# Two loads of v issued behind two transposes instead of ahead of them, on the queue of SyncE, in a fused attention and gated feed-forward kernel

## The chip, the core and the metric

The kernel runs on one core of a Trainium2 chip. The core has five engines that run their own instruction streams: TensorE (PE in the profile, its weight loads PEld), VectorE (DVE), ScalarE (ACT), GpSimd (POOL) and SyncE (SP), which here only issues transfers. Transfers run on 16 DMA engines. The metric is the device time of one execution in microseconds (us), lower is better.

## What is computed

Eight batches of eight heads, 576 tokens, head size 64: attention that is causal by blocks of 64 tokens, then a feed-forward layer with a ReLU gate over all 4608 tokens.

```python
scores = scale * np.matmul(q, k.transpose(0, 1, 3, 2))      # (8, 8, 576, 576)
mask = block_i >= block_j                                    # blocks of 64
scores = np.where(mask, scores, -1000000000.0)
attn = exp(scores - max) / sum
attn_out = np.matmul(attn, v)
x = attn_out.transpose(0, 2, 1, 3).reshape(4608, 512)
gate = np.maximum(x @ w_gate, 0.0)                           # 512 -> 1536
val = x @ w_val
out = gate * val @ w_out                                     # 1536 -> 512
```

## The kernel before

**Tiling.** A batch has 512 "main" tokens, four chunks of 128, and 64 "tail" tokens that are kept apart. Attention runs in rounds: round r is batch r // 4, head pair r % 4. A round computes the scores transposed (keys on the partitions, queries along the row), takes the exponential on ACT into `attnT`, and in the next round multiplies by v (`head_av`, L648). A column of ones beside v gives the sum for the normalisation. The rows are then turned for the feed-forward layer.

**Rounds and the feed-forward layer.** PE alternates between a round's attention and units of the feed-forward layer of an earlier batch. The generator `ffn_gen` yields after every few matmuls; `parts(n)` (L860) takes n such steps and `ffn(n)` (L847) whole units. So a `parts` or `ffn` call in the program is a stretch of PE work, and also ACT and DVE work that belongs to it.

**Order.** The whole body stands under a manual schedule for PE, DVE, ACT, POOL and SP: each engine runs its instructions in the order in which the program issues them. Where the program puts a call, it puts its instructions at that place of every engine that the call uses. An engine waits in order: an instruction that waits holds up all behind it on its engine.

**How batch 2 gets its data.** An object `Early(2)`, `e2`, loads through SP into float32 `stage` tiles (ten of them, handed out in turn, L186), POOL casts them to bf16, and transposes by DMA bring q and k into the form that the scores need:

- `e2.load_qk`, `e2.cast_qk`, `e2.transpose(0)` and `(1)` (L397): the main tokens of q and k, into `perm`, sorted by `unpermute` (L408) into `qTm` and `kTm`.
- `e2.load_tails((0, 1))`, `e2.cast_tails` (L334 and L336) and `e2.transpose_tails` (L439 and L440): the tail tokens of q and k, into `qTt[0]` and `kTt[0]`. Two transposes by DMA, issued by SP.
- `e2.load_tails((2,))` (L309): the tail tokens of v, two loads.
- `e2.load_v_chunks(0)` and `(1)` (L290): v of the main tokens, two loads of 256 KB each, in rows of 256 bytes. `e2.cast_v_chunks` (L349) on POOL puts them into `v_bf[0]` in round 8.

The first round of batch 2 is r = 8. Its `scores_all` reads `qTt[0]` in the last of its three pieces; `scores_last(2)` reads `kTt[0]` some steps later; `head_av(8, 0)`, in round 9, is the first to read the chunks of v. The same steps for batch 3 (`e3`) are issued in round 8, straight behind these on SP: loads of q and k, tails, chunks of v, transposes. Its tails go to `qTt[1]` and `kTt[1]`, first read in round 12. From batch 4 on POOL issues the loads (`load_qkv`, L460), which cast on the way.

PSUM has eight banks: three pairs are handed out in turn by `take`, two banks hold the products with v.

Of the kernel before, what the change touches and what calls it, by code (L numbers as in the profile page):

```python
# [17 lines left out]
def kernel(  # L18
# [581 lines left out]
    def tails_av(b, hh):  # L600

        av = banks[:, AV + hh, 0:260].rearrange("p (n d) -> p n d", d=65)
        for hp in range(4):
            for c in range(NCH):
                col = 1024 * hh + 256 * hp + 64 * c
                w = (
                    attnE[:, col : min(col + 128, 2048)]
                    if c < 4
                    else attnD[b % 2][:, 64 * hp : 64 * hp + 128]
                )  # L610
                nc.tensor.matmul(
                    av[0 : w.shape[1], hp, :],
                    w,
                    v_bf[b % 2][:, c, 2 * hp + hh, :],
                    start=(hp == 0 and c == 0),
                    stop=(c == 4),
                    skip_group_check=True,
                )
# [241 lines left out]
    def parts(n):  # L860

        for _ in range(n):
            next(gen)
            part[0] += 4
            done[0] += 4
# [14 lines left out]
    with tc.manual_schedule(engines={E.PE, E.DVE, E.Activation, E.Pool, E.SP}):  # L880
# [76 lines left out]
        e1, e2, tails = Early(1), Early(2), Tails()  # L957
# [75 lines left out]
        to_xT_pe(7, (dve,), banks[:, AV])  # L1033
        parts(1)
        e2.load_tails((2,))
        parts(2)
        e2.load_v_chunks(0)
        e2.load_v_chunks(1)
        parts(1)
        tails_av(0, 0)  # L1040
        tails_av(0, 1)
        tails_of(0, xt)
# [5 lines left out]
        e2.cast_tails((pool, pool))  # L1048
        parts(2)
        e2.transpose_tails()  # L1050
        parts(1)
        e2.unpermute(1, (dve, pool))
        for r in range(8, 4 * B):
# [79 lines left out]
```

## Time and profile before

| | |
|---|---|
| median of 3 runs | 368.88 us (367.63 to 368.9) |
| the profiled execution | 368.08 us, of which the span is 366.3 us |
| granted TensorE clock, mean | 0.998 |
| busy share of the span | PE 97%, DVE 45%, ACT 46%, POOL 31% |
| transfers | 51.02 MB in 136579 packets, 139 GB/s over the span |

The profile shows one execution. Times are us from the start of the span. A line of a time view gives start, length, engine, the line in the kernel, operation, tile written <- tile read, and the count of instructions; in brackets stands how long the engine was idle before it and what ended that. SPq, POOLq and ACTq are the queues of the engines that issue transfers; the length there is that of the issue, not of the transfer. Windows list, for each stretch, the busy time of PE, PEld, DVE, ACT and POOL, then the granted clock, the busy share of the DMA engines and GB/s; that share can go over 1, since several packets overlap on an engine. The share of the DMA engines by slice (40 slices of 9.2 us, in tenths) shows where transfers are dense:

```profile
PE   7899999989999999999999999999999999999995
POOL 5777854535888306800590032000000000000000
DMA  8999997799999999986899939173200130020013
GB/s 251 308 374 380 365 238 242 142 234 245 194 185 137 142 169 94 188 85 119 102 172 86 149 79 128 28 136 78 75 16 18 47 102 1 3 86 29 2 39 104
```

The place of the change is in slices 7 and 8 (64 to 82 us).

### The profile page before, as it was taken

Reading aid. Unit: us, or ns where it says so; the run is one execution under the profiler, and the core shown is the slowest. Engines: PE = TensorE matmul, PEld = TensorE weight load, DVE = VectorE, ACT = ScalarE, POOL = GpSimd, SP = SyncE. Lnnn points to the kernel's source line nnn. Section 1 sums busy time; section 2 is a strip of 40 time slices with the busy share of each in tenths; the row PEclk is TensorE's granted clock in tenths of the full one; section 3 lists DMA queues with packets and bytes.
Section 4 is the critical chain, followed back from the end, with each engine's and each line's share of the span. In section 5 each row is a group of like instructions: output and inputs, shape, how many; then the busy total and the mean of one; then the engine's idle time right before and its main releaser. Section 6 shows DMA issues by size and latency. Waiting matters only on the chain.

```text
span 366.3 us, 7450 instructions
## 1 busy us (share of the span) xinstructions
PE 354.4 (97%) x2944; PEld 187.6 (51%) x2983; DVE 165.7 (45%) x327; ACT 167.6 (46%) x266; POOL 112.9 (31%) x161
## 2 busy tenths in 40 slices
PE   7899999989999999999999999999999999999995
PEld 3544456545555455555555555555555544444443
DVE  4834446556465543444344443544344424333432
ACT  5924528456756653565346543654264303302310
POOL 5777854535888306800590032000000000000000
PEclk9999999999999999999999999999999999999999
DMA  8999997799999999986899939173200130020013
GB/s 251 308 374 380 365 238 242 142 234 245 194 185 137 142 169 94 188 85 119 102 172 86 149 79 128 28 136 78 75 16 18 47 102 1 3 86 29 2 39 104
DMA packets 136579, 51.02 MB, mean 139 GB/s; under 512 B 117472, under 2 KB 127456, under 8 KB 136544
## 3 DMA queue, kind: packets, MB, share of 16 engines
q1 hardware_dynamic: 74880, 34.29, 40.9%
q0 software_dynamic: 56384, 7.08, 37.0%
q10 hardware_dynamic: 5280, 9.18, 7.2%
q8 instruction: 23, 0.38, 0.5%
q14 instruction: 12, 0.10, 0.1%
HBM read 37.75 MB, written 9.44 MB: 129 GB/s over the span
## 4 chain that ended last, share of the span: by engine, by line
PE 85%; DMA 3%; issue 3%; POOL 2%; ACT 2%; SPq 2%; DVE 1%; POOLq 0%; DVEq 0%; ACTq 0%
PE banks L790 42%; PE banks L820 23%; PE banks L648 7%; PE banks L749 6%; PE banks L514 5%; DMA stage<-in_v_dram 2%; ACT attnT L520 2%; PE banks L869 1%; SPq L290 1%; DMA qTt<-q_bt 1%; POOL q_bf L316 1%; DVE xnat L593 1%; POOL k_bf L316 1%; PE banks L424 1%; PE banks L693 0%
## 5 line engine op out<-in xcount | busy, mean ns | idle before, releaser
L520 ACT ACTIVATE attnT<-banks 128x1024 bf16<-128x1024 f32 (+1 forms) x118 | 85.0, 805 | 56.2 <-PE banks L514 44.7
L799 ACT ACTIVATE gate_sb<-banks 128x512 bf16<-128x512 f32 x96 | 57.8, 603 | 93.0 <-PE banks L790 92.8
L820 PE MATMUL banks<-wo,hT 128*128 128x512 bf16 (+1 forms) x432 | 96.4, 373 | 1.0 <-ACT attnT L520 0.4
L804 DVE TENSOR_TENSOR hT<-gate_sb,banks 128x512 bf16<-128x512 bf16 x96 | 65.8, 687 | 69.8 <-PE banks L790 67.0
L790 PE MATMUL banks<-xT,wv 128*128 128x512 bf16 x331 | 86.6, 379 | 0.3
L790 PE MATMUL banks<-xT,wg 128*128 128x512 bf16 x319 | 85.9, 379 | 0.9
L820 PEld LDWEIGHTS <-hT 128*128 128x128 bf16 x444 | 42.4, 98 | 46.3 <-issue 0.5
L790 PEld LDWEIGHTS <-wv 128*128 128x128 bf16 x384 | 37.6, 98 | 45.2
L790 PEld LDWEIGHTS <-wg 128*128 128x128 bf16 x384 | 36.2, 98 | 40.2 <-issue 0.2
L832 DVE COPY ob<-banks 128x512 f32<-128x512 f32 (+1 forms) x37 | 25.0, 676 | 53.1 <-PE banks L820 53.0
L460 POOL DMA_DIRECT2D v_bf<-in_v_dram x16 | 14.5, 919 | 67.2 <-PE banks L648 66.6
L648 PE MATMUL banks<-v_bf,attnT 128*128 128x65 bf16 x792 | 33.2, 194 | 0.0
L648 PEld LDWEIGHTS <-attnT 128*128 128x128 bf16 x792 | 29.0, 98 | 7.3 <-issue 0.6
L514 PE MATMUL banks<-qTm,kTm 64*128 64x512 bf16 (+3 forms) x256 | 24.8, 299 | 1.7 <-ACT attnT L520 1.1
L593 DVE TENSOR_TENSOR xnat<-banks,recip 128x640 bf16<-128x640 f32 (+2 forms) x35 | 25.8, 737 | 1.4 <-DVE recip L592 0.2
L514 PEld LDWEIGHTS <-kTm 64*128 64x128 bf16 x512 | 17.1, 94 | 12.8 <-issue 4.7
L592 DVE RECIPROCAL recip<-banks 128x10 f32<-128x10 f32 (+3 forms) x37 | 7.8, 211 | 32.8 <-PE banks L648 29.7
L460 POOL DMA_DIRECT2D k_bf<-in_k_dram x16 | 14.3, 911 | 1.6 <-DMA v_bf<-in_v_dram 1.6
L460 POOL DMA_DIRECT2D q_bf<-in_q_dram x16 | 14.4, 934 | 0.0
L579 DVE MEMSET attnT<- 64x192 uint32 x25 | 5.5, 218 | 19.4 <-ACT attnT L520 16.4
L763 DVE TENSOR_TENSOR hT<-gate_sb,banks 128x512 bf16<-128x512 bf16 x12 | 7.7, 683 | 13.6 <-PE banks L749 13.6
L790 PE MATMUL banks<-xTt,wg 128*128 128x512 bf16 x48 | 12.3, 379 | 0.1
(104 smaller groups left out, 250.1 us busy)
## 6 DMA issues: line engine op xcount, KB each, us to landing
out_dram<-ob ACTq DMA_DIRECT2D x32, 256.0 KB, 2.3
stage<-in_moe_w_gate_dram SPq DMA_DIRECT2D x6, 512.0 KB, 9.0
stage<-in_moe_w_val_dram SPq DMA_DIRECT2D x6, 512.0 KB, 9.8
stage<-in_q_dram SPq DMA_DIRECT2D x6, 512.0 KB, 6.8
stage<-in_k_dram SPq DMA_DIRECT2D x6, 512.0 KB, 8.1
stage<-in_moe_w_out_dram SPq DMA_DIRECT2D x6, 512.0 KB, 10.5
stage<-in_v_dram SPq DMA_DIRECT2D x8, 256.0 KB, 4.8
q_bf<-in_q_dram POOLq DMA_DIRECT2D x16, 128.0 KB, 6.3
```

The lines of the kernel that those rows point to most:

```text
L460: nc.gpsimd.dma_start(dst, src[b, :, 128 * c : 128 * c + n, :].rearrange("h p d -> p h d"),)
L514: nc.tensor.matmul(o, kTm[b % 2][ps, c, hp, :], x, start=True, stop=True)
L520: nc.scalar.activation(out, sc, AF.Exp, scale=scale)
L592: nc.vector.reciprocal(recip, av[:, :, :, 64])
L593: nc.vector.tensor_tensor(out=out, in0=av[:, :, :, 0:64], in1=recip.to_broadcast([rows, heads, n, 64]), op=AX.mult,)
L648: nc.tensor.matmul(av[:, 0, p, :], w, vb[:, c, h, :], start=(p == 0), stop=(c == p), skip_group_check=True,)
L749: nc.tensor.matmul(out[key][:, f % 2, :], (wg, wv)[t][i][:, c, fo : fo + 128], x[:, c, :], start=(c == 0), stop=(c == 3),)
L790: nc.tensor.matmul(out[f][:, t, :], (wg, wv)[t][i][:, c, fo : fo + 128], x[:, c, :], start=(c == 0), stop=(c == 3),)
L799: nc.scalar.activation(gate[f], out[f][:, 0, :], AF.Relu)
L804: nc.vector.tensor_tensor(out=h, in0=gate[f], in1=out[f][:, 1, :], op=AX.mult)
L820: nc.tensor.matmul(ops[:, g, 0 : n1 - n0], hT[f][:, 128 * s : 128 * (s + 1)], wo[i][:, f % 4, n0:n1], start=(f == 0), stop=(f == 11),)
L832: nc.vector.tensor_copy(ob, ops[:, g, 0 : n1 - n0])
```

## The change

Batch 2's two calls that load v in chunks move behind the call that transposes its tails. The stretches of PE work around them are the same: `parts(2)` and `parts(1)` become `parts(3)`.

```diff
         e2.load_tails((2,))
-        parts(2)
-        e2.load_v_chunks(0)
-        e2.load_v_chunks(1)
-        parts(1)
+        parts(3)
         tails_av(0, 0)
...
         e2.cast_tails((pool, pool))
         parts(2)
         e2.transpose_tails()
+        e2.load_v_chunks(0)
+        e2.load_v_chunks(1)
         parts(1)
         e2.unpermute(1, (dve, pool))
         for r in range(8, 4 * B):
```

The functions that these calls reach:

```python
def load_v_chunks(self, g):
    st = self.st["c", g] = new_stage(1024)
    for i in range(2):
        s0 = 256 * g + 128 * i
        nc.sync.dma_start(
            st[:, 512 * i : 512 * i + 512].rearrange("p (h d) -> p h d", h=8),
            v[self.b, :, s0 : s0 + 128, :].rearrange("h p d -> p h d"),
        )
...
def transpose_tails(b, q_t):
    nc.sync.dma_start_transpose(qTt[b % 2], q_t)
    nc.sync.dma_start_transpose(
        kTt[b % 2], k_bt[b % 2].rearrange("p h n -> p (h n)")
    )
```

All six transfers are issued by SP. No other engine's stream changes.

## The prediction

> **What bounds the kernel now.** I read the page first, then the waits of the matmul engine, then the chain of waits around the place of the change, and last the transfers.
>
> ```profile
> span 366.3 us, 7450 instructions
> PE 354.4 (97%) x2944; PEld 187.6 (51%) x2983; DVE 165.7 (45%) x327; ACT 167.6 (46%) x266; POOL 112.9 (31%) x161
> PE 85%; DMA 3%; issue 3%; POOL 2%; ACT 2%; SPq 2%; DVE 1%; POOLq 0%; DVEq 0%; ACTq 0%
> ```
>
> ```profile
> PE banks L514 <- DMA qTt<-q_bt: 1.6, 1, 1.6
> ```
>
> PE is busy for 354.4 of 366.3 us. The line by itself is the whole answer to "what did PE wait for from 76 us to the end": one wait, for batch 2's qTt. After it the chain of work runs through PE alone. So time can be won behind 76 us only at that one wait, and an end of the kernel can move later only if something new stops PE.
>
> ```profile
> 61.08 0.90 PE L514 MATMUL banks<-qTt,kTm 64*128 64x64 bf16 x32
> ...
> 76.30 0.72 PE L514 MATMUL banks<-qTm,kTm 64*128 64x512 bf16 x8
> 78.59 0.29 PE L514 MATMUL banks<-qTt,kTm 64*128 64x64 bf16 x8 [1.57 <-DMA qTt<-q_bt]
> ...
> 85.18 0.59 PE L648 MATMUL banks<-v_bf,attnT 128*128 128x65 bf16 x14
> ...
> 105.64 0.28 PE L514 MATMUL banks<-qTt,kTm 64*128 64x64 bf16 x8
> ```
>
> This is PE in order of time (start, length, line, operation). The scores of round 8 begin at 76.30 and run out of work at 77.02; the eight matmuls on batch 2's tail queries start at 78.59, after 1.57 us idle. 85.18 is the first product with batch 2's v. 105.64 is the same eight matmuls of batch 3.
>
> ```profile
> 67.14 0.41 POOL k_bt L336
> ...
> 70.11 1.73 SPq L290
> ...
> 73.13 1.28 SPq L290
> ...
> 74.58 3.96 DMA qTt<-q_bt
> ```
>
> The chain of waits says why. The cast that the transposes need ends on POOL at 67.55, but SP comes to them only at 74.58, because the v chunks (L290) stand ahead from 70.11.
>
> ```profile
> 68.76 1.31 SPq L309 DMA_DIRECT2D stage<-in_v_dram  x2
> 70.11 4.30 SPq L290 DMA_DIRECT2D stage<-in_v_dram  x4
> 74.58 1.69 SPq L439 DMA_TRANSPOSE qTt<-q_bt  x1
> 76.38 1.20 SPq L440 DMA_TRANSPOSE kTt<-k_bt  x1
> 77.62 0.58 SPq L257 DMA_DIRECT2D stage<-in_q_dram  x1
> ...
> 97.95 1.43 SPq L439 DMA_TRANSPOSE qTt<-q_bt  x1
> 99.48 2.22 SPq L440 DMA_TRANSPOSE kTt<-k_bt  x1
> ```
>
> SP's queue: two tail loads of v, four chunk loads, the two transposes of batch 2, then the loads of batch 3; its two tail transposes come at 97.95 and 99.48. Time from issue to landing, in this order: the last chunk load, the two transposes of batch 2, batch 3's first load of q, the two transposes of batch 3.
>
> ```profile
> stage<-in_v_dram SPq DMA_DIRECT2D x1, 256.0 KB, 5.0
> qTt<-q_bt SPq DMA_TRANSPOSE x1, 4.0
> kTt<-k_bt SPq DMA_TRANSPOSE x1, 2.6
> stage<-in_q_dram SPq DMA_DIRECT2D x1, 512.0 KB, 4.1
> qTt<-q_bt SPq DMA_TRANSPOSE x1, 6.3
> kTt<-k_bt SPq DMA_TRANSPOSE x1, 8.1
> ```
>
> **The change, part by part.** No instruction is added or removed. On SP four loads and two transposes trade places; the order of every other engine stays, and so does the order in which stage buffers are handed out, so no load gets another buffer to wait for.
>
> *The transposes, moved up.* They need the casts (over at 67.55) and the old qTt read out (the row at 61.08, over by 62). Neither is late at 70.11, so SP issues them there, right behind the v tails. From 74.58 to 77.62 the pair took 3.04 us with its gaps. Landing is 2.6 to 6.3 us behind the issue by the nearest rows; I take 4.0, which had the chunk loads ahead, so 74.1, and 76.4 at the worst. Both lie ahead of 77.02, so this wait goes whole: **1.57 us**. Matmuls behind it need nothing else that is late: ACT's exponentials are further down.
>
> The Trainium skill, DMA: Bandwidth & Descriptors, section Queues, rings and completion order, says that a DMA's semaphore increment is a strongly ordered write that lands only after every earlier write of that engine. By that rule qTt's landing carried the chunk loads ahead of it, and the trace agrees as far as kTt's 2.6 is shorter than qTt's 4.0; with 2.6 the landing would be at 72.7, and the sum the same.
>
> *The chunk loads, moved down.* First issue 70.11 + 3.04 = 73.15. From the first issue to the last landing they took 73.13 + 5.0 - 70.11 = 8.0 us, so the last lands at 81.2. Below that: the first issue took 1.73 us of SP where an even share of the four is 1.08; without that excess 80.5. Above: with batch 3's transposes as the measure (97.95 to 101.70, 3.75 us), 81.9. Then POOL casts:
>
> ```profile
> 78.22 1.04 POOL L349 CAST v_bf<-stage 128x1024 bf16<-128x1024 f32 x1 [1.13 <-DMA stage<-in_v_dram]
> 81.82 1.04 POOL L316 CAST q_bf<-stage 128x1024 bf16<-128x1024 f32 x1 [2.56 <-DMA stage<-in_q_dram]
> ```
>
> 81.2 + 0.1 + 1.04 = 82.3 (81.6 to 83.0). The first v product, moved up by the gain, stands at 85.18 - 1.57 = 83.6. The cover is 1.3 us (0.6 to 2.0): no cost. Without cover each microsecond would cost one. POOL's next cast, 81.82 before, starts some 0.5 later, and catches up in POOL's gaps.
>
> *ACT.* Its last exponential of round 8 cannot move up by the whole 1.57:
>
> ```profile
> 78.92 1.02 ACT L520 ACTIVATE attnT<-banks 128x1024 bf16<-128x1024 f32 x1 [0.19 <-PE banks L514]
> ```
>
> It waited 0.19 only, since ACT had the earlier ones to do until 78.73, and so ends at 79.75 instead of 79.94. ACT can then be 1.57 - 0.19 = 1.38 us behind PE's new pace at most. PE feels a late gate only when it wants that unit's pair of banks again, and there are three pairs: no cost.
>
> *What is late next: batch 3.* Its loads start behind the same six transfers, and SP reaches them at the same 77.62 (77.62 is 70.11 + 4.30 + 3.04 with gaps, in either order). What changes is what the DMA engines still have to do then.
>
> ```profile
> 78.00:79.00 1.00, 0.41 (x14) 0.36 (x14) 0.00 (x0) 0.81 (x2) 0.78 (x1) 1.00 0.47 73
> 79.00:80.00 1.00, 1.00 (x21) 0.77 (x19) 0.14 (x1) 0.94 (x1) 0.26 (x1) 1.00 0.23 62
> 80.00:81.00 1.00, 0.95 (x6) 0.43 (x5) 0.93 (x3) 0.21 (x1) 0.00 (x0) 1.00 1.08 383
> ```
>
> The last three columns are PE's granted clock, the DMA engines' share and GB/s. The engines had room at 78 to 80 (0.47, 0.23), and ran full from 80 with batch 3's loads. In the changed kernel the chunks, landing by 81.2, fill that room, and batch 3's first load comes behind them: 512 KB at 383 GB/s is 1.4 us, so it lands at about 82.1 if its data follow at 80.7, against 77.62 + 4.1 = 81.7 before. Call this shift s: 0.4. With chunks at 80.5 it is zero; if nothing of the room were used, it would be the whole 3.04.
>
> It matters because PE now comes earlier to batch 3's tails. qTt landed at 97.95 + 6.3 = 104.25 and was read at 105.64: 1.39 spare. kTt landed at 99.48 + 8.1 = 107.6 and its weights were loaded at 108.7:
>
> ```profile
> L551 PEld LDWEIGHTS <-kTt x4: 97/98/98, 108.7 to 109.0; 128*128 128x128 bf16 x4
> ```
>
> That is 1.10 spare. A PE that is 1.57 ahead uses both up. With s = 0.4: qTt at 104.65 against 104.07, PE waits 0.58; kTt at 108.0 against 107.71, it waits 0.29. Kept: 1.57 - 0.58 - 0.29 = **0.70**; in general 1.10 - s, and never over 1.57. Later rounds gave no wait before, and I see none that 0.7 us would make.
>
> **Sum.** The profiled execution took 368.08 (366.3 its span); minus 0.7 is 367.4. The shown median, 368.88, lies 0.8 above it (runs from 367.63 to 368.9). I take the middle of the two, 368.4, as the time before: **367.7**.
>
> **Rivals.** (1) *The whole 1.57 is kept*: batch 3's tails land earlier than worked out, since chunks need less than 8.0 us behind the shorter transposes, or since the loads that POOL issues for batch 4 come at another moment. For it: those transposes took 6.3 and 8.1 with POOL's transfers beside them, 4.0 and 2.6 without. Against: both queues start later by the same late landings. Time 366.8.
>
> (2) *Slower*: the late chunks push all of batch 3, and its tail transposes become the new, longer wait of PE at 105.64 and 108.7. For it: the engines run full from 80 us, and 8.1 against 2.6 shows what neighbours cost a small transpose there. Against: the room at 78 to 80 is 0.53 + 0.77 = 1.3 us of the engines, to set against the 3.04. It decides from s = 1.1; with the whole 3.04 the kernel loses 3.04 - 1.10 = 1.9, time 370.3.
>
> The skill's same page, Rules for kernel authors, advises to issue a DMA early and to wait on it late; for the chunks and all behind them the change does the reverse. With 3.04 us given up to 1.3 of cover at the v products, the trace does not bear that out here as a loss; by the rule the time would be that of (2) or (3).
>
> (3) *PE waits for the v chunks* instead, at the product of 85.18. With the cast over at 84.1 it would wait 0.5, and batch 3 takes no more than before, since PE has then 1.07 of lead, within the spare of 1.10: 367.3. For a loss the last chunk must land at 84.1, 6 us later than before, and no row gives that.
>
> That the change does not do what it says I exclude: the cast is over 2.6 us before SP is free.
>
> **Numbers.** Forecast 0.50; whole gain 0.20; batch 3 late 0.24; chunks late 0.06. The forecast's own range, for s from 0 to 0.8, is 367.3 to 368.1, and with the spread of the runs 367.0 to 368.6. The 8-in-10 range goes to both neighbours: 366.4 (whole gain with a fast base) to 369.7 (s of some 2.4). A half per cent, 1.8 us, is about what a measurement of this kernel can tell from no change. Faster by over that: most of the whole gain when the time before is at 368.9 (0.14), the forecast's edge (0.07), some of (3): 0.22. Slower by over that: the far part of (2), 0.20. Within: 0.58.
>
> **What would show it.** In the changed profile: SP issues L439 at about 70.1 and L290 from about 73.1; PE's wait for qTt at 77.0 is gone; the casts L349 end by 82.3 and the product at 83.6 starts without a wait; PE's waits list shows, if anything, qTt and kTt of batch 3 near 104 and 108, 0.9 us together. Wrong it would be if PE still waits at 77.0, if L648 waits for POOL near 83.6, or if the waits near 104 and 108 are none (rival 1) or over 1.6 (rival 2).

## The result and the profile after

| | before | after |
|---|---|---|
| median | 368.4 us, 6 runs, 367.63 to 373.48 | 373.24 us, 6 runs, 371.05 to 375.0 |
| profiled execution | 368.08 us, span 366.3 | 372.03 us, span 370.2 |
| granted TensorE clock, mean | 0.998 | 0.995 |

The ratio of the times is 1.0134, interval 1.0089 to 1.0178: **slower by 1.3%**, where 367.7 us was forecast. Ratios here leave out executions that lie over 1.5% above the fastest of their kernel; medians and ranges have them all.

The page of the changed kernel; the last line is the chain that ended last, by engine.

```profile
span 370.2 us, 7450 instructions
PE 355.7 (96%) x2944; PEld 188.0 (51%) x2983; DVE 165.6 (45%) x327; ACT 167.5 (45%) x266; POOL 113.3 (31%) x161
...
PEclk9999999999989999999999999999999999999999
...
PE 81%; DMA 13%; DVE 1%; SPq 1%; ACT 1%; issue 1%; POOL 0%; DVEq 0%; ACTq 0%; POOLq 0%
```

The chain now runs through transfers for 13% of the span, against 3%. PE is 1.3 us longer busy on the same 2944 instructions, and the twelfth slice of its clock (102 to 111 us) stands at 8. What PE waited for from 68 us to the end:

```profile
PE banks L514 <- DMA qTt<-q_bt: 4.1, 1, 4.1
PE banks L820 <- issue: 0.2, 1, 0.2
```

Still a single wait for a qTt, but 4.1 in place of 1.6. PE in order of time shows that it's another batch's:

```profile
76.23 0.72 PE L514 MATMUL banks<-qTm,kTm 64*128 64x512 bf16 x8
76.79 0.28 PE L514 MATMUL banks<-qTt,kTm 64*128 64x64 bf16 x8
...
83.37 0.59 PE L648 MATMUL banks<-v_bf,attnT 128*128 128x65 bf16 x14
...
103.28 0.72 PE L514 MATMUL banks<-qTm,kTm 64*128 64x512 bf16 x8
108.06 0.40 PE L514 MATMUL banks<-qTt,kTm 64*128 64x64 bf16 x8 [4.07 <-DMA qTt<-q_bt]
...
110.04 2.98 PE L820 MATMUL banks<-wo,hT 128*128 128x512 bf16 x10 [0.22 <-issue]
112.85 0.28 PE L551 MATMUL banks<-qTt,kTt 128*128 128x64 bf16 x4
```

At batch 2 the tail scores (76.79) follow at once: qTt, issued at 70.17, landed 3.2 us later (4.0 had been taken), the wait of 1.57 is gone, and the product with the moved chunks (83.37) doesn't wait either. PE then leads the old kernel by 1.8 us at 103.28 (105.09 there). The lead ends at batch 3's tail scores, 108.06 against 105.64. In the kernel before, the four matmuls of L551 behind them stand at

```profile
108.92 0.28 PE L551 MATMUL banks<-qTt,kTt 128*128 128x64 bf16 x4
```

So the changed kernel is 2.42 behind at L514 and 3.93 behind at L551, which is the whole difference of the spans (3.9). The missing 1.51 between them is the clock (with a pause of 0.22 us at 110.04), in windows of the changed kernel (last columns: granted clock, DMA share, GB/s):

```profile
104.00:108.06 4.06, 0.00 (x1) 0.00 (x0) 0.00 (x0) 1.76 (x3) 2.64 (x4) 0.98 2.04 152
108.06:111.40 3.34, 3.12 (x28) 1.88 (x29) 1.93 (x4) 1.02 (x1) 1.57 (x3) 0.51 2.91 153
111.40:113.00 1.60, 1.60 (x13) 0.77 (x12) 0.41 (x3) 0.00 (x0) 1.60 (x3) 1.00 2.41 180
```

PE stands still for 4.06 us and then runs at half its clock for 3.3 us.

Why qTt is late, on SP's queue of the changed kernel:

```profile
70.17 2.09 SPq L439 DMA_TRANSPOSE qTt<-q_bt  x1
72.37 1.20 SPq L440 DMA_TRANSPOSE kTt<-k_bt  x1
73.61 3.10 SPq L290 DMA_DIRECT2D stage<-in_v_dram  x4
76.76 1.47 SPq L257 DMA_DIRECT2D stage<-in_q_dram  x1
...
85.95 5.79 SPq L290 DMA_DIRECT2D stage<-in_v_dram  x4
...
97.83 1.97 SPq L397 DMA_TRANSPOSE perm<-k_bf  x1
99.90 1.72 SPq L439 DMA_TRANSPOSE qTt<-q_bt  x1
101.72 1.57 SPq L440 DMA_TRANSPOSE kTt<-k_bt  x1
```

And the times from issue to landing of batch 3's two tail transposes:

```profile
qTt<-q_bt SPq DMA_TRANSPOSE x1, 8.1
kTt<-k_bt SPq DMA_TRANSPOSE x1, 9.0
```

The two kinds of transfers changed places as the diff says. SP reaches batch 3's loads 0.86 us *earlier* than before (76.76 against 77.62), but its tail transpose 1.95 later (99.90 against 97.95), and that takes 8.1 to land in place of 6.3. Landing at 108.0 instead of 104.25 makes 3.75 us; 0.4 had been forecast.

### The profile page after: what moved, and what is told of

Its sections match the earlier page's. It is cut to its first block, busy times and chain, and to the rows that moved or that the text cites. A ratio compares the mean times of both kernels' runs of the same rounds, so it can differ in the third digit from the quotient of the medians.

```text
span 370.2 us, 7450 instructions
## 1 busy us (share of the span) xinstructions
PE 355.7 (96%) x2944; PEld 188.0 (51%) x2983; DVE 165.6 (45%) x327; ACT 167.5 (45%) x266; POOL 113.3 (31%) x161
## 4 chain that ended last, share of the span: by engine, by line
PE 81%; DMA 13%; DVE 1%; SPq 1%; ACT 1%; issue 1%; POOL 0%; DVEq 0%; ACTq 0%; POOLq 0%
PE banks L790 45%; PE banks L820 22%; PE banks L648 7%; PE banks L514 5%; DMA stage<-in_k_dram 4%; DMA stage<-in_moe_w_out_dram 3%; DMA stage<-in_moe_w_val_dram 3%; DMA qTt<-q_bt 2%; SPq L280 1%; ACT attnT L520 1%; DMA stage<-in_v_dram 1%; PE banks L611 1%; DVE xnat L593 0%; PE banks L693 0%; POOL k_bf L316 0%
## 5 line engine op out<-in xcount | busy, mean ns | idle before, releaser
L514 PE MATMUL banks<-qTm,kTm 64*128 64x512 bf16 (+3 forms) x256 | 24.9, 299 | 1.7 <-ACT attnT L520 1.1
L514 PEld LDWEIGHTS <-kTm 64*128 64x128 bf16 x512 | 17.2, 94 | 15.1 <-issue 7.2
L514 PE MATMUL banks<-qTt,kTm 64*128 64x64 bf16 x256 | 8.5, 191 | 4.2 <-DMA qTt<-q_bt 4.1
```

Source lines behind the costliest of these rows:

```text
L514: nc.tensor.matmul(o, kTm[b % 2][ps, c, hp, :], x, start=True, stop=True)
```

## The experiments

Three things had to be told apart: the new order of the transfers, the earlier PE, and the clock. The kernels fall into four groups. Each ratio is to the kernel before, run beside on the same chip. Of the letters in the expectations, A stands for the moved transfers (the chunks, and the neighbours that the transposes then meet), D for the lead of PE by itself, F for the fetches of instructions, H for the stores.

**The neighbours of the transposes.** In the changed kernel, POOL's first load for batch 4 waits until batch 3's kTt has landed (so all of POOL's loads for batch 4 do).

```diff
-        nc.sync.dma_start_transpose(
+        tail_T[b] = nc.sync.dma_start_transpose(
...
-                nc.gpsimd.dma_start(
+                ld = nc.gpsimd.dma_start(
...
+                if (b, t, c) == (4, 0, 0):
+                    after(ld, tail_T[3])
```

> The changed kernel, but POOL's first load for batch 4 waits until batch 3's kTt has landed. Theory A (batch 3's tail transposes are late because its loads queue on the DMA engines behind the chunks that were moved, and then fall among POOL's loads for batch 4, which stretch 4 us of landing to 8): qTt of batch 3 is issued at about 99.9 as in the changed kernel but lands within 3 to 4.5 us, at 103 to 104.4; PE waits there for under 0.5 us instead of 4.07, the clock stays at 1.00, and the time is 0.995 to 0.999 of before. Theory B (SP alone issues them too late, neighbours do not matter): the landing stays 8 us behind the issue, PE waits 3 us or more, ratio 1.010 or more.

Median 371.93 us, ratio 1.0095 (1.0062 to 1.0129). Landing of batch 3's tail transposes, and PE:

```profile
qTt<-q_bt SPq DMA_TRANSPOSE x1, 4.6
kTt<-k_bt SPq DMA_TRANSPOSE x1, 3.6
```

```profile
104.87 0.29 PE L517 MATMUL banks<-qTt,kTm 64*128 64x64 bf16 x8 [0.77 <-DMA qTt<-q_bt]
```

```profile
140.26 0.72 PE L517 MATMUL banks<-qTm,kTm 64*128 64x512 bf16 x8 [2.02 <-DMA kTm<-k_bf]
```

The issue is as late as ever (100.19), yet the landing takes 4.6 and 3.6 instead of 8.1 and 9.0: it's POOL's loads beside them that stretch it. Most of the wait goes. The time doesn't come back, since batch 4's loads, now starting at 105.42 and no longer at 97.27, make a wait of 2.02 at 140 us. (The profiled execution, 370.08 us, is the shortest of the four; what the longer ones waited for is in no trace.) In this kernel the delay can be put at batch 3 or at batch 4, and neither has room for it. The same edit in the kernel before:

> The kernel before, with POOL's first load for batch 4 waiting until batch 3's kTt has landed (the edit of e1 without the change). Theory A: batch 3's qTt, issued at about 98, lands within 4.6 us instead of 6.3, at about 102.5; PE does not wait there. Batch 4's loads start near 103 instead of 96, so its kTm may come late: a wait of 0.5 to 1.5 us near 140 and a ratio of 1.001 to 1.004; without it 0.999 to 1.001. Theory B (neighbours do not matter): the landing stays 6.3 us behind the issue.

367.81 us, ratio 0.9993 (0.9965 to 1.002): no difference. The tail transposes land in 3.2 and 2.6 us, the wait at batch 2 stays (1.40), and batch 4 makes none, though POOL's loads for it start only at 106.26.

Next, batch 3's tail transposes ahead of its second pair of main ones, in the changed kernel and in the one before:

```diff
                 e3.transpose(0)
-                e3.transpose(1)
                 e3.transpose_tails()
+                e3.transpose(1)
```

> The changed kernel, with batch 3's two tail transposes issued between its two pairs of main transposes instead of behind them. Theory A and theory B alike: they are issued about 2.5 to 4 us earlier (near 95.5), land near 100 to 101, ahead of PE's 103.99, so PE does not wait there and the 1.57 us won at batch 2 is kept: ratio 0.995 to 0.998. If the second pair of main transposes takes over the delay (read by DVE near 111), DVE or PE shows a new wait near 111 to 120 and the ratio is over 1.

> The kernel before, with batch 3's tail transposes issued between its two pairs of main transposes (the edit of e3 without the change). PE's wait of 1.57 us at batch 2 stays and nothing else waited, so both theories give no change: ratio 0.998 to 1.002. It tells whether what e3 keeps comes from this edit by itself.

In the changed kernel: 368.49 us, ratio 1.0019 (0.9979 to 1.0058), with single times from 366.55 to 372.01. qTt is issued at 96.87, lands in 4.2, and batch 3 has no wait; batch 4 has 0.5 and 0.2. In the kernel before: 367.91, ratio 0.997 (0.9936 to 1.0004), with the wait at batch 2 still there (1.47). So the lateness of this one transfer carries most of the 1.3%; the gain that was forecast, 0.2% of the time, is too small for these intervals to show or to exclude.

**The clock.** In the changed kernel, 36 matmuls of 256 columns ahead of batch 3's tail scores, into columns that are written again behind them; PE works through most of its wait.

```diff
+        sc = scores(b, hp, pair(), [(0, 2, True)])
+        if r == 12:
+            for n in range(36):
+                nc.tensor.matmul(
+                    sc[:, n % 2, 256:512].rearrange("p (j n) -> p j n", j=2),
+                    kTt[0][:, 0, :],
+                    kTt[0][:, 0:1, :].to_broadcast([128, 2, 128]),
...
```

> The changed kernel with 36 matmuls of 256 columns on constants (0.108 us each at full clock, 3.9 us) put on PE just ahead of batch 3's tail matmuls; their results are overwritten. Theory C (the half clock behind 108 comes from PE's 4 us of idle time): the granted clock stays at 1.00 from 104 to 114, and the kernel ends about 1.5 us earlier than the changed one: ratio about 1.009 where the changed kernel has 1.013. Rival (the clock falls for another reason, such as the load ahead of it): the clock falls all the same and the ratio is 1.013 or more.

371.66 us, ratio 1.0097 (1.0075 to 1.012). In windows:

```profile
108.45:110.47 2.02, 0.00 (x0) 0.02 (x1) 0.00 (x0) 0.00 (x0) 0.62 (x1) 1.00 2.26 156
110.47:112.00 1.53, 1.53 (x27) 1.04 (x27) 0.58 (x2) 1.02 (x1) 0.27 (x1) 1.00 1.92 150
```

qTt lands later still (110.4), but PE has idled for 2.02 only, and the clock stays at 1.00. The half clock comes from the idle time, not from the transfers or the place.

**The order, or the lead?** First the new order without the lead: the changed kernel with 15 such matmuls in round 8, for about the 1.57 us that PE had waited there.

```diff
+        if r == 8:
+            for n in range(15):
+                nc.tensor.matmul(
...
```

> The changed kernel with 15 matmuls of 256 columns (1.6 us) put on PE ahead of batch 2's tail matmuls in round 8, so that PE, ACT's stores and all that follows PE have no lead over the kernel before; results overwritten. Theory A: batch 3's qTt still lands near 108 and PE, which comes to it at 105.6, waits 2 to 2.7 us; under the 3.4 or so at which the clock would fall it stays at 1.00; ratio 1.005 to 1.008. Theory D (PE's lead makes the landing late, by moving stores and POOL's loads forward into the transposes): the landing goes back to 104 to 105, no wait, ratio 0.998 to 1.002.

368.78 us, ratio 1.0034 (1.0007 to 1.0062). SP's queue and PE:

```profile
97.68 1.27 SPq L397 DMA_TRANSPOSE perm<-k_bf  x1
99.06 1.49 SPq L439 DMA_TRANSPOSE qTt<-q_bt  x1
```

```profile
105.55 0.72 PE L514 MATMUL banks<-qTm,kTm 64*128 64x512 bf16 x8
106.35 0.29 PE L514 MATMUL banks<-qTt,kTm 64*128 64x64 bf16 x8
```

The issue is 1.11 later than before (99.06 against 97.95), and the transpose lands in 7.2 us, at 106.3. Some 0.4 of that is no effect of the order: this execution runs later from ahead of the change's place on (SP's tail loads of v at 69.15, before 68.76). PE, with no lead, comes at about that moment. The waits list shows nothing, but the two groups of L514 stand 0.80 apart where the kernel before has 0.55, so some 0.25 us are lost there. One thing besides the lead differs: with 15 more instructions, PE's instruction fetches fall between 80 and 81, 91 and 92, and 104 and 105 us, and before between 82 and 83, and 94 and 95. Now the lead without the new order: the kernel before, in which the tail scores of round 8 read batch 1's tail queries, which are there in time. No transfer is moved; batch 2's scores of these queries are other numbers.

```diff
-                x = qTm[b % 2][ps, c:4, hp, :] if main else qTt[b % 2][ps, hp, :]
+                x = qTm[b % 2][ps, c:4, hp, :] if main else qTt[1 if (b, hp) == (2, 0) else b % 2][ps, hp, :]
```

> The kernel before, but the tail scores of round 8 take batch 1's tail queries, which lie ready, instead of batch 2's; SP's order is that of before. PE then has the lead of 1.57 us without any transfer moved. Theory A (the moved chunks make batch 3 late): batch 3's qTt lands near 104.3 as before, PE comes at 104.0 and waits 0.2 to 0.5 us there and at kTt; ratio 0.995 to 0.999. Theory D (PE's lead alone makes the landing late): it lands at 106 to 108, PE waits 2 to 4 us, ratio 1.003 to 1.013.

372.42 us, ratio 1.0104 (1.0055 to 1.0153): PE's wait is taken away with nothing else, and the kernel is slower by 1%. PE, SP's queue, and the landing:

```profile
109.39 0.40 PE L514 MATMUL banks<-qTt,kTm 64*128 64x64 bf16 x8 [5.34 <-DMA qTt<-q_bt]
```

```profile
78.29 1.54 SPq L257 DMA_DIRECT2D stage<-in_k_dram  x1
...
85.02 7.05 SPq L290 DMA_DIRECT2D stage<-in_v_dram  x4
...
100.01 2.07 SPq L439 DMA_TRANSPOSE qTt<-q_bt  x1
```

```profile
qTt<-q_bt SPq DMA_TRANSPOSE x1, 9.3
kTt<-k_bt SPq DMA_TRANSPOSE x1, 9.5
```

With SP's order untouched, qTt is issued 2.06 us later than before and takes 9.3 us instead of 6.3. An earlier PE makes the transfers of the *next* batch later. That had no place in the prediction.

Two other ways to shift the load between the transfers. In the first, qTt stays ahead of the chunks in the changed kernel and kTt goes behind them. The second adds to it batch 3's tails ahead, as above.

```diff
-        e2.transpose_tails()
+        nc.sync.dma_start_transpose(qTt[0], e2.tl)
         e2.load_v_chunks(0)
         e2.load_v_chunks(1)
+        nc.sync.dma_start_transpose(kTt[0], k_bt[0].rearrange("p h n -> p (h n)"))
```

> Half of the change: qTt's transpose ahead of the chunk loads, kTt's behind them. PE's wait at batch 2 is gone as in the changed kernel, but the chunks are pushed back by some 2.2 us instead of 3.4. Theory A: batch 3's loads land about 1 us earlier than in the changed kernel, its qTt by 106 to 107, PE waits 2 to 3 us, the clock stays up: ratio 1.002 to 1.007. Theory D: PE's lead is the same, so the wait and the ratio are those of the change, 1.010 to 1.015.

> The edits of e7 and e3 together: qTt ahead of batch 2's chunks, kTt behind them; batch 3's tail transposes between its main pairs. Theory A: chunks are pushed back by 2.2 us only and batch 3's tails have 4 us more: no wait at batch 2 or 3, ratio 0.994 to 0.998. Rival E (the transfers between 96 and 135 us set the pace, and any lead of PE is given back at batch 4): PE waits 1 us or more for kTm or qTt of batch 4 near 138 and the ratio is 0.998 to 1.005.

The first: 369.79 us, with single times from 366.98 to 374.69, ratio 1.001 (0.996 to 1.0059), nearer to A than to D; over all ten the mean is 370.03, against 368.56 before. The profiled one, 372.69, has a wait of 3.04 us for batch 3's qTt. The second: **366.89 us, ratio 0.996 (0.9933 to 0.9987)**, the lowest median that was found. But three of its 13 executions took over 372, and over all of them the mean is 368.22, against 368.49 before: hardly a gain. The profiled one is among the three (373.49), and shows where the time goes:

```profile
141.28 1.25 PE L514 MATMUL banks<-qTm,kTm 64*128 64x512 bf16 x8 [4.24 <-DMA kTm<-k_bf]
```

No wait at batches 2 and 3, but 4.24 at batch 4, with half the clock behind it. Batch 3's chunks behind all its transposes, with the tails between the two main pairs, meet the same place:

```diff
-                e3.load_v_chunks(0)
-                e3.load_v_chunks(1)
...
                 e3.transpose(0)
-                e3.transpose(1)
                 e3.transpose_tails()
+                e3.transpose(1)
+                e3.load_v_chunks(0)
+                e3.load_v_chunks(1)
```

> The changed kernel, with the same done for batch 3 in full: its v chunks go behind all its transposes, and its tail transposes between the two main pairs. All theories: batch 3's qTt is issued by about 92 and lands by 98, 6 us ahead of PE, so PE does not wait there. The chunks land near 105 and are cast by 107, ahead of their first product at about 107.5 to 109, with little to spare; if that spare is gone PE waits there. POOL's loads for batch 4 start behind those casts, near 107 instead of 97, so that kTm of batch 4 may be the next wait, near 138. Ratio 0.996 to 1.000 without a new wait, 1.003 to 1.010 with one.

372.83 us, ratio 1.0094 (1.0055 to 1.0133): no wait at batch 3's tails, but 3.83 for batch 4's kTm at 141.4, and 0.26 for v.

One miss: batch 2's chunks issued by ACT, in the kernel before.

```diff
-                nc.sync.dma_start(
+                (nc.scalar if self.b == 2 else nc.sync).dma_start(
...
```

> The kernel before, but batch 2's four chunk loads are issued by ACT instead of SP, at the same place of the program; SP then comes to the transposes at about 70.1 with no load put behind them. Theory A (what hurts batch 3 is that the moved chunks hold the DMA engines when its loads come): chunks keep their old time, batch 3's loads are issued 3 to 4 us earlier than in the changed kernel, its qTt lands by 104, PE waits at neither place, and the kernel keeps most of 1.57 us: ratio 0.995 to 0.999. Theory D (PE's lead alone makes batch 3 late): qTt lands at 106 or later and PE waits 2 us or more there, ratio 1.005 or more. ACT loses about 1.4 us to issuing, which its idle time hides.

373.72 us, ratio 1.0103 (1.0019 to 1.0187). It doesn't test what it was made for, since the four issues held ACT itself:

```profile
67.76 8.36 ACTq L290 DMA_DIRECT2D stage<-in_v_dram  x4
```

PE then waited 5.01 us for ACT's exponentials at 77.3.

**What carries the lead into the transfers?** Two suspects follow PE's progress: the fetches of its instructions, and the stores of the feed-forward layer. The fetches are on the instruction queue. In the kernel with the lead alone, a fetch falls on SP's load of k at 78.29; this is the queue's share of the stretch from 78.2 to 78.8:

```profile
q8 instruction: 1, 0.02, 11.4%
```

The kernel before has no such packet in that stretch, and its same issue takes 0.51, not 1.54:

```profile
78.25 0.51 SPq L257 DMA_DIRECT2D stage<-in_k_dram  x1
```

On SP's queue this row alone carries nothing on: the chunk loads of batch 3 start at 85.02, before at 84.94. These four then take 7.05 us instead of 5.87, and so end 1.26 later. And an issue can be long without a fetch: the changed kernel's of 1.47 us at 76.76 has none beside it.

To move the fetches, 11 warming matmuls of 512 columns at the start were cut into 44 of 128, in the kernel before and in the one with the lead alone:

```diff
         for _ in range(n):
+            for j in range(4):
                 nc.tensor.matmul(
-                bank.rearrange("p (j n) -> p j n", j=4),
+                    bank[:, 128 * j : 128 * j + 128],
...
```

> The kernel before, with its 11 warming matmuls of 512 columns at the start cut into 44 of 128 columns: the same columns, 66 more instructions on PE ahead of everything. PE's instruction fetches (256 instructions each) then come about 3 us earlier, near 79, 91 and 104 us as in the changed kernel; order, lead and stores are those of before. Theory F (a fetch in the flight of batch 3's transposes makes them late): qTt of batch 3 lands at 105.7 or later instead of 104.25 and PE waits there for up to 3 us; ratio 1.002 to 1.010. Theory G (the fetches do not matter; the stores or other transfers that follow PE do): it lands at 103.5 to 104.8, no wait, ratio 0.998 to 1.002.

> e9 (the lead alone) with the same 66 instructions more at the start; fetches near 76, 88 and 101. Theory F: the landing of batch 3's qTt moves by a microsecond or more against e9's 109.4, most likely down, since the fetch at 104 is gone from its flight: 105 to 107, wait 1 to 3 us, ratio 1.000 to 1.007. Theory G: as e9, landing at 107.5 or later, ratio 1.008 to 1.015.

373.66 us, ratio 1.0103 (1.0062 to 1.0144), and 376.88, ratio 1.0201 (1.0136 to 1.0265). The edit also made the start later (2.57 us at round 8 in the first), and the fetches didn't fall where they were meant to. Both got slower, and the first not where either theory had it: it has no wait at batch 3, but its old wait at batch 2 grew to over 3 us, with a clock of 0.56 over the next 3.3 us.

```profile
82.69 0.29 PE L514 MATMUL banks<-qTt,kTm 64*128 64x64 bf16 x8 [3.10 <-DMA qTt<-q_bt]
```

The second has a wait of 6.21 at batch 3. The pair is no test of the fetches, for or against.

The stores: the four of batch 1's main rows left out, in the kernel with the lead alone and in the changed one. Those rows of the output aren't written.

```diff
     def put(j, s, ob, n0, n1):
+        if j == 1:
+            return
```

> e9 (PE's lead alone) without the four stores of batch 1's main output rows, which ACT issues between 94 and 110; those rows are not written. Theory H (the stores, moved 1.7 us ahead, hold up batch 3's transposes): qTt of batch 3 is issued near 98 and lands by 105, PE waits under 1 us, the clock stays up, ratio 0.994 to 1.000. Theory F (the instruction fetches do): issue near 99 to 100 and landing at 107 or later as in e9, wait 3 us or more, ratio 1.004 to 1.012.

> The changed kernel without the same four stores; those rows are not written. Theory H: its qTt of batch 3 lands 2 to 3 us earlier than 108, at 105 to 106, PE waits 1 to 2 us, ratio 0.998 to 1.003. Theory F: lands within 1 us of 108, wait 3 us or more, ratio 1.006 to 1.013.

367.04 us, ratio 0.9981 (0.9945 to 1.0018), and 368.24, ratio 0.9983 (0.9954 to 1.0012): by the times, the loss goes in both. But the traces don't show how. Each kernel's profiled execution was one of its longest (371.85 and 371.71), and in both the wait is there; in the first of them:

```profile
107.47 0.29 PE L514 MATMUL banks<-qTt,kTm 64*128 64x64 bf16 x8 [3.49 <-DMA qTt<-q_bt]
```

Leaving out 1 MB of stores also relieves the DMA engines, whoever leads. The kernel before without them was not run, so what leaving them out is worth by itself isn't known. Nor do the rows put all four where the expectation has them: with the lead alone they are issued at 97.04, 101.02, 109.90 and 140.00 (the one at 94.62 is batch 0's last, and stays). SP's chunk loads, over at 92.07 with the 1.26 us of delay, stand ahead of the first, so this part can't come from them; the rest of the 2.06 and the long landing could. So it stays open whether the stores do harm because they come earlier or only because they are there.

## Why the prediction was wrong

**Right: where the gain was, and the change's own cover.** The only wait of PE behind 68 us went whole. The chunks were in time: they landed by 80.7 where 81.2 was expected, and their last cast:

```profile
80.72 1.04 POOL L349 CAST v_bf<-stage 128x1024 bf16<-128x1024 f32 x1 [1.28 <-DMA stage<-in_v_dram]
83.51 1.04 POOL L316 CAST q_bf<-stage 128x1024 bf16<-128x1024 f32 x1 [1.74 <-DMA stage<-in_q_dram]
```

It ends at 81.76, ahead of 83.37. Rival 3 fell.

**Right: the place of the danger.** The prediction named batch 3's qTt and kTt with spares of 1.39 and 1.10, and the loss from s = 1.1. Its own formula, 1.10 - s, gives -2.65 with the measured 3.75; at L514 the kernel is 2.42 behind. (kTt, landing at 110.7, was read only at 112.85, and made no wait.) It was rival 2 that came true, with a chance of 0.24.

**Wrong: the shift s, 0.4 where 3.75 came.** This is the step "what is late next: batch 3": the issue was 1.95 later and the landing took 1.8 longer. Two things went wrong in it.

First, *the room at 78 to 80 us*. It was filled, as forecast, but not at the 383 GB/s that the estimate of q's load took. In windows of the changed kernel:

```profile
78.00:79.00 1.00, 0.95 (x6) 0.46 (x5) 0.89 (x3) 1.00 (x2) 0.59 (x1) 1.00 1.36 236
79.00:80.00 1.00, 1.00 (x6) 0.42 (x5) 1.00 (x2) 1.00 (x2) 0.45 (x1) 1.00 1.11 190
```

Full engines moved 190 to 236 GB/s there. So batch 3's first q, in time for its cast at 82.1 by the estimate, was cast at 83.51; before it was 81.82. The kernel with the order and no lead has it at 83.73, the one with the lead and no order at 81.86: this part is the order's. From there it is carried down SP's queue, to an issue 1.11 later and a landing 2.0 later (106.3 against 104.25) in the kernel without the lead, or 1.6 without the 0.4 by which that execution runs late from the start. By the prediction's own formula s = 1.6 is a loss of 0.5 us, and rival 2, not the forecast.

Second, *the timetable of the transfers was taken as fixed*. "Both queues start later by the same late landings" was the coupling allowed for, other moments of POOL's loads stood only in rival 1, as a gain, and the landing time of 6.3 was carried over. The experiment with the lead alone shows that PE's lead by itself shifts batch 3's transposes, by 5.1 us (109.3 against 104.25) in its profiled execution. In the changed kernel, what lies between the landing of the order alone (105.9 to 106.3) and 108.0 goes with it. The times would add (order without lead 0.3% slower, lead without order 1.0%, both together 1.3%), but the landings, each from one execution, don't: 1.6 and 5.1 us later alone, 3.75 together.

**Missing: the clock.** Half clock behind a wait of 4.07 us costs 1.51, more than a third of the loss of the spans. The prediction had no term for it: rival 2's worst case, a loss of 1.9 us, is by its own figures a wait of 3.22 us for qTt (104.25 + 3.04 against 104.07), priced as idle time alone. No slice of the page before showed a clock at half. The trace of the kernel before shows 1.57 us idle with the clock at 1.00 on both sides, and waits of 2.02 left it at 1.00, too; so the loss isn't in proportion to the lateness: it jumps somewhere between waits of 2.02 and 3.04 us.

The Trainium skill, TensorE: Matmul & The Clock Gate, Part 1: The HAM clock gate, states that the clock falls to half after at least one idle window, about 3.4 us, and that the window runs freely; the traces agree in kind, though here 3.04 us were enough. By that rule rival 2's wait of 3.22 us lies just under a window; by the waits measured here it needed a term for the clock.

**Shown, argued, open.** Shown: that qTt of batch 3 is what PE waits for, that POOL's loads stretch its landing, that idle time halves the clock, that the lead alone suffices for the loss. Argued from single rows: that an instruction fetch lengthens an issue, and how much of the delay is the order's. Open: through what PE's lead reaches the chunk loads and transposes of batch 3 (85 to 109 us). The times without stores point to the stores, the rows up to 92 us away from them, and the trace to no single transfer; and why single executions of one of these kernels lie 5 us apart was seen in no trace, since each kernel has only one.

## What to carry to other kernels

A wait that is removed gives back no more than the spare of the next deadline that transfers set, so look up each later one (landing against first use) before counting the gain: here it was 1.1 to 1.4 us at batch 3, and what was pushed past it met the next at batch 4. Where the DMA engines are full, don't carry a landing time over as a constant: move one thing alone on the chip, the order without the lead and the lead without the order. In this kernel, count a wait of PE of 3 us or more as the wait plus the half clock behind it (1.51 us behind 4.07).

## What the hardware showed that was not expected

- **Half clock after idle time.** PE idle for 1.57 (before) and 2.02 us (two kernels) kept a clock of 1.00. Behind idle times of 3.04, 3.10, 3.49, 3.58, 3.83, 4.07, 4.24, 5.01, 5.34 and 6.21 us in other kernels it was granted 0.50 to 0.68 over the next 2.7 us. This is the shortest of them, qTt alone ahead of the chunks, in windows:

```profile
104.48:107.52 3.04, 0.00 (x0) 0.00 (x0) 0.00 (x0) 1.76 (x3) 2.12 (x3) 0.81 1.70 155
107.52:113.00 5.48, 5.26 (x33) 2.64 (x34) 2.34 (x6) 1.02 (x1) 2.68 (x4) 0.50 2.29 173
```

  The clock falls already within the wait (0.81), and stays at half for 5.48 us.
- **A small transpose beside POOL's loads.** Over all kernels here, batch 3's tail transposes took 5.1 to 10.3 us from issue to landing when they were issued behind the first of POOL's loads for batch 4, and 2.4 to 4.6 when they were issued ahead of it or those loads were held back.
- **The same issue can take over twice as long.** Four loads of 256 KB took SP 3.10, 4.30, 5.79 or 7.05 us, and ACT 8.36.
- **One profiled execution can mislead.** With the lead and no stores it took 371.85, against a median of 367.04; with qTt and batch 3's tails ahead, 373.49 against 366.89. What such a trace shows is what the long executions do.
